# Two MLPs behind cluster attention on one core: the last two heads' values are multiplied with the tokens in columns

## The chip, the cores and the metric

One core of one Trainium2 chip runs the whole program. The metric is the device time of an execution in microseconds (us). TensorE is called PE here (its weight loads PEld), VectorE DVE, ScalarE ACT, GpSimd POOL, and SP is the engine that issues most DMAs. A line number such as L578 is that of the kernel before the change.

## The reference, cut to what matters

```
# q, k, v: 2 batches x 8 heads x 768 tokens x 64; 16 centroids per head
mask = q_assign[:, :, :, None] == k_assign[:, :, None, :]     # same nearest centroid
scores = where(mask, q @ k.T / 8, -1e9);  scores -= max(scores, -1)
attn = exp(scores);  attn = attn / (sum(attn, -1) + 1e-9)
x = (attn @ v) as 1536 tokens x 512                           # 8 heads side by side
x = gelu-like MLP(x): 512 -> 2048 -> 512
out = gated MLP(x):   512 -> 1536 (gate and value) -> 512
```

The 16 pairs of batch and head are called heads 0 to 15 below; heads 14 and 15 are the last two of batch 1.

## The kernel before

All five engines run an order that is written out by hand: each engine takes its instructions in the order of the Python code, and semaphores hold it where an operand or a buffer is not ready. Numbers are held as two float32r parts, a high one and a low rest, and a product is three matmuls (high by high, high by low, low by high).

A head goes through these steps. `next_smax` (matmul L531, maximum on DVE L536) finds the largest score of each query token of the *following* head, in 12 steps of 384 columns. `mneg` and `mrow` turn the maxima into one row of the query operand: a DVE reduce, a PE transposition into the bank `ps_x`, a copy on ACT and a DMA. `scores(h, c, n)` computes the scores of 128 key tokens (c, 0 to 5) by 384 query tokens (n, 0 and 1) with two matmuls (L578) into one of three banks `ps_s`, and ACT takes the exponential into `p` (L585). `pv(h, c)` (L594) then multiplies by the values: `p` is the stationary operand, 128 tokens at a time, and 65 columns of values (the 65th is ones, for the sums) stream, in float32. `norm` divides on DVE, with tokens on the partitions, and `to_x` (L625) transposes two heads at a time on PE back to features on the partitions and splits the result into `xh` (ACT, L631) and `xl` (DVE, L632).

In head 14 one `next_smax` stands behind each `scores`; in head 15 the twelve `scores` stand alone, since no head follows. After all scores of a head come its six `pv`. `take(4)` moves the decoding of weight tiles along (L81 and L83 on ACT, four steps L85 to L97 on DVE), and `run` splits decoded tiles into `sp` (ACT L160, DVE L161).

Then the first MLP starts. `m1_s1(0, f)` is one block of `h` matmuls (L167) for batch 0, in a part of 512 and one of 256 tokens, each into one of the two banks `ps_m`; tanh on ACT (L193), a multiply on DVE (L196) that frees the bank, a cast on ACT (L198) and a rest on DVE (L205) follow. Two blocks are computed ahead, and the last `to_x` stands within the first; then blocks of `a` matmuls and of `h` matmuls alternate to the end.

Of the kernel before, what the change touches and what calls it, by code (L numbers as in the profile page):

```python
# [8 lines left out]
F32 = mybir.dt.float32  # L9
# [16 lines left out]
def tile_cluster_attention_two_mlps(ctx: ExitStack, tc: tile.TileContext, qk, v, cen, w1, w2, wg, wv, w3, out):  # L26
# [18 lines left out]
    def pool(stack, name, bufs, **kw):  # L45
        return stack.enter_context(tc.tile_pool(name=name, bufs=bufs, reuse_waits="tile", **kw))
# [238 lines left out]
    with ExitStack() as att:  # L285
# [5 lines left out]
        ps_x = pool(att, "ps_x", 1, space=PSUM)  # L291
        ps_o = pool(att, "ps_o", 2, space=PSUM)
        ps_s = pool(att, "ps_s", 3, space=PSUM)
        qk_stack = ExitStack()
        qk_p = pool(qk_stack, "qk", 1)

# [7 lines left out]

        q2_t = [(qk1_p if i == FIRST else qk_p).tile([128, 2, S], F32R, name=f"q2_{i}") for i in range(NQK)]
        k2_t = [(qk1_p if i == FIRST else qk_p).tile([128, 2, S], F32R, name=f"k2_{i}") for i in range(NQK)]
# [263 lines left out]
        def scores(h, c, n):  # L572
            if n == 0:
                p_t[h, c] = p_p.tile([128, S], F32, tag="p", name="p")
            at = slice(n * HALF, (n + 1) * HALF)
            ps = ps_s.tile([128, 512], F32, tag="s", name="st")[:, 0:HALF]
            for a, rows in ((0, 2 * D), (1, MROW + 1)):
                nc.tensor.matmul(  # L578
                    out=ps,
                    lhsT=k2(h)[0:rows, a, c * 128:(c + 1) * 128],  # L580
                    rhs=q2(h)[0:rows, a, at],
                    start=(a == 0),
                    stop=(a == 1),
                )
# [119 lines left out]


        EARLY = 3
        for h in range(NH):
            more, ahead = h + 1 < NH, h + 4 < NH
            maxima = list(steps) if more and h > 1 else []
            for step in () if h == 0 else steps[2 * EARLY:] if h == 1 else steps:  # L710
                scores(h, *step)
                if maxima:
                    next_smax(h + 1, maxima)
            if h == 0:
                load_qk(5)
# [11 lines left out]
            if h == NH - 1:  # L727
                qk_stack.close()
                sp_p = pool(ctx, "sp", 6, side="right")
                g_p = pool(ctx, "gp", 3, side="right")  # L730
                w_pools.append(pool(ctx, "wd1", LATE, side="right"))
            for c in range(SC):
                if h or c:
                    pv(h, c)
                if more and c == 0:
                    if h > 1:
                        mrow(h + 1)
                    load_v(h + 1)
                    if ahead:
                        if h > 0:  # L740
                            hi_k(h + 4)
                            lo_q(h + 4, nc.gpsimd if h == 1 else nc.vector)
                            lo_k(h + 4, nc.gpsimd if h == 1 else nc.vector)
# [30 lines left out]
                if h == NH - 1 and c > 0:  # L774
                    run([], [[("1", 0)], [("1", 1), ("2", 0)], [("1", 2)], [("2", 1)], []][c - 1], 0)
# [8 lines left out]
            if h == NH - 1:  # L784
                norm(h)
# [76 lines left out]
```

## Time and profile before

| | before |
|---|---|
| median of 3 runs | 836.12 us (835.83 to 837.07) |
| profiled execution | 836.04 us, of which the trace spans 834.2 us |
| PE busy | 99% of the span, 4736 matmuls |
| DVE, ACT, POOL busy | 72%, 54%, 4% |
| granted TensorE clock, mean | 0.999 |

A matmul counts as busy from its start until its result is written, and matmuls overlap, so 99% does not say that PE is at its peak: the distance from one start to the next tells what a matmul costs. Times in the trace are counted from the start of the span. Head 14's first score matmul starts at 238.68, the first `h` matmul at 266.56 and the first `a` matmul at 276.36.

### The profile page before, as it was taken

To read this page: it belongs to the slowest core of one execution; us is meant where nothing else is said; L and a number is where in the kernel's file an instruction comes from. 1 tells how busy PE (TensorE), PEld (TensorE's weight loads), DVE (VectorE), ACT (ScalarE), POOL (GpSimd) and SP (SyncE) were. 2 spreads that over 40 slices of the span, in tenths; PEclk is the share of its full clock that TensorE was granted. 3 is DMA by queue.
4 is the path that set the end of the run, shared out by engine and by line. 5 is a ranking of instruction groups with operands and counts; after the bars stand their busy time and mean duration, and the time that the engine had idled before them with its cause. 6 is when DMAs were issued, how large, how long until landed. Compare 5 with 4: busy or idle time off the path is not lost.

```text
span 834.2 us, 12291 instructions
## 1 busy us (share of the span) xinstructions
PE 826.6 (99%) x4736; PEld 732.9 (88%) x4736; DVE 604.0 (72%) x1131; ACT 448.6 (54%) x828; POOL 36.4 (4%) x48
## 2 busy tenths in 40 slices
PE   8999999999999999999999999999999999999998
PEld 6999999999999888888888888888888888888886
DVE  7888898898973588888977776798965544555452
ACT  7847766766754465656654545565633333333331
POOL 8530000000000000000000000000000000000000
PEclk9999999999999999999999999999999999999999
DMA  6124123111211133333222222122201000010001
GB/s 127 31 81 110 37 55 88 35 54 50 66 50 47 51 101 112 116 102 112 91 76 83 70 98 80 51 79 99 75 1 51 1 0 1 1 51 0 1 1 50
DMA packets 26242, 49.79 MB, mean 60 GB/s; under 512 B 14548, under 2 KB 14632, under 8 KB 26184
## 3 DMA queue, kind: packets, MB, share of 16 engines
q1 hardware_dynamic: 25240, 47.24, 18.9%
q10 hardware_dynamic: 944, 1.77, 0.6%
q8 instruction: 37, 0.61, 0.3%
q14 instruction: 21, 0.17, 0.1%
HBM read 45.12 MB, written 3.15 MB: 58 GB/s over the span
## 4 chain that ended last, share of the span: by engine, by line
PE 94%; DVE 4%; ACT 1%; issue 1%; ACTq 0%; DVEq 0%
PE h L167 39%; PE a L167 28%; PE pv L594 13%; PE st L578 7%; PE smax L531 4%; DVE nm L536 1%; PE sims L447 1%; PE xt L625 0%; PE warm L366 0%; DVE k L349 0%; DVE q L343 0%; ACT p L585 0%; DVE oT L504 0%; DVE T L484 0%; DVE mx L482 0%
## 5 line engine op out<-in xcount | busy, mean ns | idle before, releaser
L167 PE MATMUL h<-xh,sp 128*128 128x512 f32 (+1 forms) x1088 | 313.9, 365 | 0.5 <-DVE t L196 0.5
L167 PEld LDWEIGHTS h<-xh,sp 128*128 128x128 f32 x1088 | 198.3, 189 | 33.8 <-issue 0.7
L167 PE MATMUL h<-xl,sp 128*128 128x512 f32 (+1 forms) x544 | 198.4, 365 | 0.0
L167 PE MATMUL a<-g,sp 128*128 128x512 f32 (+1 forms) x768 | 139.6, 338 | 0.0
L196 DVE SCALAR_TENSOR_TENSOR t<-t,h 128x512 f32<-128x512 f32 x100 | 60.0, 600 | 104.1 <-ACT t L193 104.1
L594 PEld LDWEIGHTS pv<-v,p 128*128 128x128 f32 x1152 | 134.8, 192 | 0.1
L167 PEld LDWEIGHTS a<-g,sp 128*128 128x128 f32 x768 | 120.0, 189 | 16.8
L594 PE MATMUL pv<-v,p 128*128 128x65 f32 x1152 | 134.3, 273 | 0.0
L193 ACT ACTIVATE t<-h 128x512 f32<-128x512 f32 x100 | 52.7, 527 | 144.8 <-PE h L167 144.8
L161 DVE TENSOR_TENSOR sp<-w,sp 128x512 fp32r<-128x512 f32 x172 | 115.4, 687 | 10.3 <-ACT sp L160 10.0
L167 PEld LDWEIGHTS h<-xl,sp 128*128 128x128 f32 x544 | 102.7, 189 | 16.2
L585 ACT ACTIVATE p<-st 128x384 f32<-128x384 f32 x192 | 89.9, 492 | 35.7 <-PE st L578 30.1
L160 ACT CAST sp<-w 128x512 fp32r<-128x512 f32 x172 | 101.9, 617 | 9.2 <-PE a L167 8.4
L167 PE MATMUL a<-sp,g 128*128 128x512 f32 x432 | 103.6, 389 | 0.0
L536 DVE TENSOR_REDUCE nm<-smax 128x1 f32<-128x384 f32 x192 | 98.0, 554 | 6.0 <-PE smax L531 5.6
L578 PE MATMUL st<-q,k 128*128 128x384 f32 (+1 forms) x384 | 98.4, 348 | 0.1
L167 PEld LDWEIGHTS a<-sp,g 128*128 128x128 f32 x432 | 81.1, 188 | 16.8
L205 DVE TENSOR_TENSOR g<-t,g 128x512 fp32r<-128x512 f32 x100 | 60.4, 604 | 28.7 <-ACT g L202 24.8
L202 ACT CAST g<-t 128x512 fp32r<-128x512 f32 x36 | 22.4, 623 | 97.4 <-DVE t L201 97.4
L578 PEld LDWEIGHTS st<-q,k 128*128 128x128 f32 (+1 forms) x384 | 67.3, 190 | 4.4 <-ACT p L585 2.7
L531 PE MATMUL smax<-k,q 80*128 80x384 f32 x192 | 62.9, 344 | 0.5 <-ACT q L507 0.2
L201 DVE TENSOR_TENSOR t<-t,h 128x512 f32<-128x512 f32 x36 | 24.8, 688 | 36.6 <-PE h L167 35.7
(99 smaller groups left out, 640.4 us busy)
## 6 DMA issues: line engine op xcount, KB each, us to landing
raw<-in_w SPq DMA_DIRECT2D x44, 512.0 KB, 3.2
raw<-in_wg SPq DMA_DIRECT2D x12, 512.0 KB, 3.1
raw<-in_wv SPq DMA_DIRECT2D x12, 512.0 KB, 3.5
st<-in_qk SPq DMA_DIRECT2D x15, 384.0 KB, 5.5
v<-in_v SPq DMA_DIRECT2D x16, 192.0 KB, 3.1
out<-osb ACTq DMA_DIRECT2D x6, 256.0 KB
out<-osb SPq DMA_DIRECT2D x6, 256.0 KB, 2.4
q<-oT SPq DMA_DIRECT2D x7, 48.0 KB, 2.2
```

What stands on the lines that cost most here:

```text
L160: lambda: nc.scalar.copy(t[:, 0, :], w),
L161: lambda: nc.vector.tensor_tensor(out=t[:, 1, :], in0=w, in1=t[:, 0, :].bitcast(F32), op=ALU.subtract),
L167: nc.tensor.matmul(out=out_ps, lhsT=lhs[a], rhs=rhs[b], start=(start and j == 0), stop=(stop and j == 2), **kw)
L193: nc.scalar.activation(t, hs[0], ACTF.Tanh, scale=tanh_scale)
L196: nc.vector.scalar_tensor_tensor(out=t, in0=t, scalar=1.0, in1=hs[0], op0=ALU.add, op1=ALU.mult)
L201: nc.vector.tensor_tensor(out=t, in0=t, in1=hs[1], op=ALU.mult)
L205: nc.vector.tensor_tensor(out=g[:, 1, at], in0=t, in1=g[:, 0, at].bitcast(F32), op=ALU.subtract)
L531: nc.tensor.matmul(out=ps, lhsT=q2(h)[0:ONE + NC, 1, c * 128:(c + 1) * 128], rhs=k2(h)[0:ONE + NC, 1, n * HALF:(n + 1) * HALF],)
L536: nc.vector.tensor_reduce(out=nm_t[h][:, c, n:n + 1], in_=ps, axis=AX.X, op=ALU.max)
L578: nc.tensor.matmul(out=ps, lhsT=k2(h)[0:rows, a, c * 128:(c + 1) * 128], rhs=q2(h)[0:rows, a, at], start=(a == 0), stop=(a == 1),)
L585: nc.scalar.activation(p_t[h, c][:, at], ps, ACTF.Exp, scale=scale)
L594: nc.tensor.matmul(out=pv_t[h][:, i, :], lhsT=p[:, i * 128:(i + 1) * 128], rhs=v_t[h % 3][:, c, :], start=(c == 0 and i == 0), stop=(c == ...
```

## The change

Only heads 14 and 15 and what follows them up to the first `a` block are changed.

- The values become the stationary operand: `split_v`, on POOL, builds a high and a low tile of 128 columns per 128 key tokens, 64 of them the values and 64 ones (zeros in the low tile). The exponentials stream: ACT copies each `p` into a high part `hi` (128x768), and POOL (head 14) or DVE (head 15) subtracts to get `lo`. `pvg` multiplies, three matmuls of 384 columns for each c and n. The result has features on 64 partitions, the sums on the other 64, and tokens in columns.
- Blocks of `pvg` stand behind the next scores: a list `todo` is worked off until two entries are left. Head 15's maxima are found two behind each `scores` of head 14, in its c = 0 to 2. `to_x` of heads 12 and 13, `mneg` and `mrow` stand among head 14's scores.
- `norm_g` divides in this layout: two DVE transposes bring the sums to columns, reciprocal, a broadcast copy on ACT, two transposes back, two multiplies. For head 14 its steps stand among head 15's scores, for head 15 among the first `m1_s1`. `split_x` takes the place of the last `to_x`, without PE.
- After the last scores, the remaining `pvg` run for n = 1 first, ACT copies that result out of its `ps_m` bank (`off_bank`), then n = 0.
- Two decodings move: from head 14, c = 1 and 4, to head 13, c = 3, and head 14, c = 5. Splits of `sp` stand behind head 15's exponentials instead of beside its `pv`. Pools are arranged so that the new tiles reuse buffers of heads 12 and 13.

```diff
@@ scores @@
             nc.scalar.activation(p_t[h, c][:, at], ps, ACTF.Exp, scale=scale)
+            if h >= NH - 2 and n == 1:
+                p = p_t.pop((h, c))
+                hi, lo = (q2_t, k2_t)[c // 2 % 2][U3][:, c % 2, :], p_p.tile([128, S], F32R, tag="p", name="lo")
+                hl_t[h, c] = hi, lo
+                nc.scalar.copy(hi, p)
+                (nc.gpsimd, nc.vector)[h % 2].tensor_tensor(out=lo, in0=p, in1=hi.bitcast(F32), op=ALU.subtract)
...
+        def pvg(h, c, low, ns=(0, 1)):
+
+            vh, vl = vs_t[h]
+            for n in ns:
+                if (h, n) not in pg_t:
+                    pl, tag = (ps_o, "o") if h % 2 == 0 else ((ps_x, "x"), (ps_m, "m"))[n]
+                    pg_t[h, n] = pl.tile([128, 512], F32, tag=tag, name="pg")[:, 0:HALF]
+                for w in (vh,) if low else (vh, vl):
+                    nc.tensor.matmul(
+                        out=pg_t[h, n], lhsT=w[:, c, :], rhs=hl_t[h, c][low][:, n * HALF:(n + 1) * HALF],
...
+        def norm_g(h):
...
+            for n in range(2):
+                nc.vector.transpose(out=d[:, n, :], in_=pg_t[h, n][sums])
+            yield
...
+            nc.vector.reciprocal(rd, rd)
+            nc.scalar.copy(d.rearrange("p n (b c) -> p n b c", c=32), rd.to_broadcast([64, 2, HALF // 32, 32]))
+            yield
+            for n in range(2):
+                nc.vector.transpose(out=r[rows, n * HALF:(n + 1) * HALF], in_=d[:, n, :])
+            yield
+            for n in range(2):
+                at = slice(n * HALF, (n + 1) * HALF)
+                nc.vector.tensor_tensor(out=x[rows, at], in0=pg_t[h, n][rows], in1=r[rows, at], op=ALU.mult)
+            yield
...
-        for at in ((NH - 4, 1), (NH - 4, 4), (NH - 3, 1), (NH - 2, 1), (NH - 2, 4)):
+        for at in ((NH - 4, 1), (NH - 4, 4), (NH - 3, 1), (NH - 3, 3), (NH - 2, 5)):
...
-        for h in range(NH):
+        for h in range(NH - 2):
...
+        maxima = list(steps)
+        todo = []
+        for h in (NH - 2, NH - 1):
+            for c in range(SC):
+                for n in range(2):
+                    scores(h, c, n)
+                    for _ in range(2 if maxima else 0):
+                        next_smax(NH - 1, maxima)
+                todo += [(h, c, False), (h, c - 1, True)] if c else [(h, c, False)]
...
+                    if c == 3:
+                        mneg(h + 1)
+                    if c == 4:
+                        mrow(h + 1)
+                    if c in (3, 4):
+                        to_x((h - 2) // 2, c - 3)
+                    take(takes.get((h, c), 0))
+                elif c > 1:
+                    next(after)
...
+                while len(todo) > 2:
+                    pvg(*todo.pop(0))
+                if h == NH - 1 and c == 1:
+                    after = norm_g(NH - 2)
...
+        last = norm_g(NH - 1)
         for i in range(2):
             for j, step in enumerate(m1_s1(0, i)):
                 step()
-                if i == 0 and j in (0, 3):
-                    to_x(NH // 2 - 1, j // 3)
+                if i == 0:
+                    next(last, None)
+                if i == 0 and j == 2:
+                    run([], [("1", 2)], 0)
+                if i == 1 and j in (0, 3):
+                    split_x(j // 3)
```

PE's order in head 14, c = 1 and 2 (`st` are the scores, `smax` the scores that are searched for head 15's maxima, `pg` the product with the values). Before:

```order
L578 MATMUL st_2860<-q2_4_118,k2_4_123 128x384 [waits Activation_49]
L578 MATMUL st_2860<-q2_4_118,k2_4_123 128x384
L531 MATMUL smax_2864<-k2_0_119,q2_0_114 128x384 [waits DVE_49]
L578 MATMUL st_2867<-q2_4_118,k2_4_123 128x384 [waits Activation_49]
L578 MATMUL st_2867<-q2_4_118,k2_4_123 128x384
L531 MATMUL smax_2871<-k2_0_119,q2_0_114 128x384 [waits DVE_49]
```

The same place on PE now (line numbers in these rows are those of the kernel they are from):

```order
L588 MATMUL st_2888<-q2_4_121,k2_4_126 128x384 [waits PE_49]
L588 MATMUL st_2888<-q2_4_121,k2_4_126 128x384
L541 MATMUL smax_2895<-k2_0_122,q2_0_117 128x384 [waits DVE_49]
L541 MATMUL smax_2898<-k2_0_122,q2_0_117 128x384 [waits DVE_49]
L632 MATMUL pg_2901<-q2_3_120,q2_2_119 128x384 [waits Activation_49,Pool_49]
L632 MATMUL pg_2901<-q2_3_120,q2_2_119 128x384 [waits Pool_49]
L632 MATMUL pg_2904<-q2_3_120,q2_2_119 128x384 [waits PE_49]
L632 MATMUL pg_2904<-q2_3_120,q2_2_119 128x384
L588 MATMUL st_2908<-q2_4_121,k2_4_126 128x384 x2
L541 MATMUL smax_2912<-k2_0_122,q2_0_117 128x384 [waits DVE_49]
L541 MATMUL smax_2915<-k2_0_122,q2_0_117 128x384 [waits DVE_49]
```

Two `smax`, each of which waits for a maximum on DVE, now stand between two pairs of scores, and the first product stands behind them in the same queue.

ACT's order in the last half of head 15 (`p` the exponentials, the casts from `p` are `hi`, `d` is the broadcast copy of head 14's reciprocal sums). Before, up to the first weight split:

```order
L585 ACTIVATE p_3019<-st_3020 128x384 [waits PE_49,Activation_49]
L585 ACTIVATE p_3019<-st_3024 128x384 [waits PE_49]
L585 ACTIVATE p_3028<-st_3029 128x384 [waits PE_49,Activation_49]
L585 ACTIVATE p_3028<-st_3033 128x384 [waits PE_49]
L585 ACTIVATE p_3037<-st_3038 128x384 [waits PE_49,Activation_49]
L585 ACTIVATE p_3037<-st_3042 128x384 [waits PE_49]
L160 CAST sp_3074<-w_1071 128x512
```

ACT now, from c = 3 to the end of head 15:

```order
L595 ACTIVATE p_3087<-st_3088 128x384 [waits PE_49]
L595 ACTIVATE p_3087<-st_3092 128x384 [waits PE_49]
L600 CAST k2_3_125<-p_3087 128x768 [waits Activation_49]
L663 COPY d_3077<-rdg_3099 64x768 [waits DMAHW7_49,DVE_49]
L595 ACTIVATE p_3109<-st_3110 128x384 [waits PE_49]
L595 ACTIVATE p_3109<-st_3114 128x384 [waits PE_49]
L600 CAST q2_3_120<-p_3109 128x768 [waits Activation_49]
L595 ACTIVATE p_3129<-st_3130 128x384 [waits PE_49]
L595 ACTIVATE p_3129<-st_3134 128x384 [waits PE_49]
L600 CAST q2_3_120<-p_3129 128x768 [waits Activation_49]
```

A cast of 768 columns now follows every two exponentials, and between c = 3 and c = 4 a copy that waits for DVE stands ahead of the last four exponentials.

DVE's order beside the first two `h` blocks (`t` and `g` are the MLP's gate; L196 frees the `h` bank). Before:

```order
L196 SCALAR_TENSOR_TENSOR t<-t,h 128x512
L205 TENSOR_TENSOR g<-t,g 128x512 [waits DMAHW7_49,DMAHW4_49,Activation_49]
L632 TENSOR_TENSOR xl_78<-xt,xh_77 128x256 [waits Activation_49]
L196 SCALAR_TENSOR_TENSOR t<-t,h 128x256
L205 TENSOR_TENSOR g<-t,g 128x256 [waits Activation_49]
```

DVE at the same place now:

```order
L196 SCALAR_TENSOR_TENSOR t<-t,h 128x512 [waits Activation_49]
L658 TENSOR_SCALAR rdg<-d 64x24 [waits DVE_49]
L662 RECIPROCAL rdg<-rdg 64x24 [waits DVE_49]
L205 TENSOR_TENSOR g<-t,g 128x512 [waits DMAHW1_49,Activation_49]
L666 STREAM_TRANSPOSE r<-d 64x384 [waits Activation_49]
L666 STREAM_TRANSPOSE r<-d 64x384
L161 TENSOR_TENSOR sp<-w,sp 128x512 [waits Activation_49]
L670 TENSOR_TENSOR xg<-pg,r 64x384 [waits DVE_49]
L670 TENSOR_TENSOR xg<-pgs,r 64x384 [waits DVE_49]
L196 SCALAR_TENSOR_TENSOR t<-t,h 128x256 [waits Activation_49]
L205 TENSOR_TENSOR g<-t,g 128x256 [waits Activation_49]
```

Between the two L196 that free the first block's two banks, DVE now has seven more instructions of head 15's division and of a weight split, where it had one.

## Rows read from the trace of the kernel before

**Rows 1.** Page, first part: busy us, share of the span, instructions.

```profile
PE 826.6 (99%) x4736; PEld 732.9 (88%) x4736; DVE 604.0 (72%) x1131; ACT 448.6 (54%) x828; POOL 36.4 (4%) x48
```

**Rows 2.** Chain that ended last, in order of time: start us, us, what.

```profile
210.17 5.95 DVE nm L536 x12
...
246.63 6.70 PE pv L594 x60
253.33 4.87 PE st L578 x24
...
263.51 0.44 PE xt L625 x4
...
265.24 0.23 PE xt L625 x2
...
270.75 0.54 issue
```

**Rows 3.** Busy time of each engine in stretches of heads 14 and 15.

```profile
core 0: us, PE busy (x) PEld busy (x) DVE busy (x) ACT busy (x) POOL busy (x), PEclk, DMA share, GB/s
238.68:245.12 6.44, 6.44 (x38) 6.44 (x38) 5.63 (x11) 5.28 (x11) 0.00 (x0) 1.00 0.00 0
245.12:253.14 8.02, 8.02 (x75) 8.02 (x74) 6.57 (x14) 3.29 (x7) 0.00 (x0) 1.00 0.48 153
...
238.68:276.36 37.68, 37.19 (x268) 34.89 (x268) 21.85 (x44) 20.34 (x43) 0.00 (x0) 1.00 0.11 34
```

**Rows 4.** Timeline of PE at the second h block and the first a block.

```profile
272.12 0.47 PE L167 MATMUL h<-xh,sp 128*128 128x512 f32 x1 [0.49 <-DVE t L196]
...
276.36 4.36 PE L167 MATMUL a<-g,sp 128*128 128x512 f32 x24
```

**Rows 5.** Timeline of ACT and DVE: start us, us, engine, line, instruction, count.

```profile
239.49 6.39 DVE L536 TENSOR_REDUCE nm<-smax 128x1 f32<-128x384 f32 x12 [1.04 <-PE smax L531]
...
246.00 0.15 DVE L611 TENSOR_SCALAR rd<-pv 128x6 f32<-128x6 f32 x1
...
246.41 0.56 DVE L613 TENSOR_TENSOR xr<-pv,rd 128x384 f32<-128x384 f32 x1
...
246.89 0.68 DVE L85 SCALAR_TENSOR_TENSOR u<-u,raw 128x512 f32<-128x512 f32 x1
...
248.79 0.69 DVE L97 CUSTOM_DVE_ANT_0 w<-m,t 128x1024 uint16<-128x1024 uint16 x1
...
253.77 4.98 ACT L585 ACTIVATE p<-st 128x384 f32<-128x384 f32 x12 [3.51 <-PE st L578]
...
263.99 0.59 ACT L631 CAST xh<-xt 128x512 fp32r<-128x512 f32 x1 [3.18 <-PE xt L625]
...
264.61 0.69 DVE L632 TENSOR_TENSOR xl<-xt,xh 128x512 fp32r<-128x512 f32 x1 [2.82 <-ACT xh L631]
...
269.57 0.60 ACT L193 ACTIVATE t<-h 128x512 f32<-128x512 f32 x1 [3.70 <-PE h L167]
...
271.29 0.68 DVE L196 SCALAR_TENSOR_TENSOR t<-t,h 128x512 f32<-128x512 f32 x1
272.00 0.62 ACT L198 CAST g<-t 128x512 fp32r<-128x512 f32 x1 [1.35 <-DVE t L196]
...
273.60 0.41 DVE L196 SCALAR_TENSOR_TENSOR t<-t,h 128x256 f32<-128x256 f32 x1
```

**Rows 6.** Groups by line, whole span: busy us, mean ns | idle before.

```profile
L338 ACT CAST k<-st 64x768 fp32r<-64x768 f32 x15 | 12.4, 830 | 0.1
L349 DVE TENSOR_TENSOR k<-st,k 64x768 fp32r<-64x768 f32 x11 | 10.5, 950 | 9.7 <-ACT k L338 9.5
L504 DVE STREAM_TRANSPOSE oT<-T 64x384 f32<-64x384 f32 x18 | 10.3, 572 | 0.7
L349 POOL TENSOR_TENSOR k<-st,k 64x768 fp32r<-64x768 f32 x5 | 9.1, 1826 | 0.4
```

**Rows 7.** Instructions on the tile k: duration ns min/median/max, start us.

```profile
L508 POOL CAST k<-oT x4: 497/530/1289, 12.4 to 24.4; 16x384 fp32r<-16x384 f32 x4
```

More of the change, by code (lines that the diff above doesn't have):

```diff
@@ L293, in tile_cluster_attention_two_mlps @@
         ps_s = pool(att, "ps_s", 3, space=PSUM)
+        qkb_stack = ExitStack()
+        qkb_p = pool(qkb_stack, "qkb", 1)
         qk_stack = ExitStack()
@@ L302, in tile_cluster_attention_two_mlps @@
         FIRST = (NH - NQK) % NQK
-        q2_t = [(qk1_p if i == FIRST else qk_p).tile([128, 2, S], F32R, name=f"q2_{i}") for i in range(NQK)]
-        k2_t = [(qk1_p if i == FIRST else qk_p).tile([128, 2, S], F32R, name=f"k2_{i}") for i in range(NQK)]
+        U2, U3 = ((NH - j) % NQK for j in (4, 3))
+        in_b = {("q", U3), ("k", U3), ("k", U2)}
+        q2_t, k2_t = (
+            [
+                (qk1_p if i == FIRST else qkb_p if (a, i) in in_b else qk_p).tile([128, 2, S], F32R, name=f"{a}2_{i}")
+                for i in range(NQK)
+            ]
+            for a in "qk"
+        )
         v_t = [acst.tile([128, SC, D + 1], F32, name=f"v_{i}") for i in range(3)]
@@ L585, in scores, with split_v @@
             nc.scalar.activation(p_t[h, c][:, at], ps, ACTF.Exp, scale=scale)
+            if h >= NH - 2 and n == 1:
[4 more added lines that the diff above has]
+                (nc.gpsimd, nc.vector)[h % 2].tensor_tensor(out=lo, in0=p, in1=hi.bitcast(F32), op=ALU.subtract)
+        hl_t = {}
+        vs_t = {}
+        def split_v(h):
+            dst = (q2_t, k2_t)[h % 2][U2]
+            vh, vl = (dst[:, i, :].rearrange("p (c d) -> p c d", d=2 * D) for i in range(2))
+            at, other = slice(0, D), slice(D, 2 * D)
+            if h % 2:
+                at, other = other, at
+            src = v_t[h % 3][:, :, 0:D]
+            nc.gpsimd.memset(vh[:, :, other].bitcast(F32), 1.0)
+            nc.gpsimd.memset(vl[:, :, other].bitcast(F32), 0.0)
+            nc.gpsimd.tensor_copy(vh[:, :, at], src)
+            nc.gpsimd.tensor_tensor(out=vl[:, :, at], in0=src, in1=vh[:, :, at].bitcast(F32), op=ALU.subtract)
+            vs_t[h] = vh, vl
@@ new lines, in tile_cluster_attention_two_mlps @@
+        pg_t = {}
+        def pvg(h, c, low, ns=(0, 1)):
[7 more added lines that the diff above has]
+                        out=pg_t[h, n], lhsT=w[:, c, :], rhs=hl_t[h, c][low][:, n * HALF:(n + 1) * HALF],
+                        start=(c == 0 and not low and w is vh), stop=(c == SC - 1 and low), skip_group_check=True,
+                    )
@@ new lines, in off_bank @@
+        def off_bank(h, n):
+            t = p_p.tile([128, S], F32, tag="p", name="pgs")[:, 0:HALF]
+            nc.scalar.copy(t, pg_t[h, n])
+            pg_t[h, n] = t
+        xg_t = []
+        def norm_g(h):
+            if not xg_t:
+                xg_t.append(xr_p.tile([128, SC, 2, D], F32, tag="xr", name="xg").rearrange("p a b d -> p (a b d)"))
+            x = xg_t[0]
+            rows, sums = slice(0, D), slice(D, 2 * D)
+            if h % 2:
+                rows, sums = sums, rows
+            d = am_p.tile([64, 2, HALF], F32, tag="oT", name="d")
+            r = p_p.tile([128, S], F32, tag="p", name="r")
+            for n in range(2):
+                nc.vector.transpose(out=d[:, n, :], in_=pg_t[h, n][sums])
+            yield
+            rd = sm_p.tile([64, 2, HALF // 32, 1], F32, tag="rdg", name="rdg")
+            nc.vector.tensor_scalar(
+                out=rd, in0=d.rearrange("p n (b c) -> p n b c", c=32)[:, :, :, 0:1],
+                scalar1=1e-9, scalar2=None, op0=ALU.add,
+            )
+            nc.vector.reciprocal(rd, rd)
[8 more added lines that the diff above has]
+            yield
@@ L587, in tile_cluster_attention_two_mlps, with split_x @@
+        def split_x(p):
+            t0, n = parts[p]
+            part, at = x_at(B - 1, p)
+            j = H // 2 - 1
+            x = xg_t[0][:, t0:t0 + n]
+            nc.scalar.copy(xh[part][:, j, at], x)
+            nc.vector.tensor_tensor(
+                out=xl[part][:, j, at], in0=x, in1=xh[part][:, j, at].bitcast(F32), op=ALU.subtract
+            )
         pv_t = {}
@@ L773, in tile_cluster_attention_two_mlps @@
                     norm(h - 1)
-                if h == NH - 1 and c > 0:
-                    run([], [[("1", 0)], [("1", 1), ("2", 0)], [("1", 2)], [("2", 1)], []][c - 1], 0)
+                if h == NH - 3 and c == 3:
+                    split_v(h + 1)
                 take(takes.get((h, c), 0))
@@ L783, in tile_cluster_attention_two_mlps @@
                         to_x((h - 3) // 2, c - 3)
-            if h == NH - 1:
-                norm(h)
+        maxima = list(steps)
[7 more added lines that the diff above has]
+                todo += [(h, c, False), (h, c - 1, True)] if c else [(h, c, False)]
+                if c == SC - 1:
+                    todo.append((h, c, True))
+                if h == NH - 2:
+                    if c == 0:
+                        norm(h - 1)
+                        load_v(h + 1)
+                    if c == 2:
+                        split_v(h + 1)
+                    if c == 3:
[7 more added lines that the diff above has]
+                    next(after)
+                if h == NH - 1 and c == SC - 1:
+                    break
+                while len(todo) > 2:
+                    pvg(*todo.pop(0))
+                if h == NH - 1 and c == 1:
+                    after = norm_g(NH - 2)
+        qk_stack.close()
+        sp_p = pool(ctx, "sp", 6, side="right")
+        run([], [("1", 0)], 0)
+        for n in (1, 0):
+            for at in todo:
+                pvg(*at, (n,))
+            if n == 1:
+                off_bank(NH - 1, n)
+        qkb_stack.close()
+        g_p = pool(ctx, "gp", 3, side="right")
+        w_pools.append(pool(ctx, "wd1", LATE, side="right"))
+        run([], [("1", 1), ("2", 0)], 0)
+        last = norm_g(NH - 1)
         for i in range(2):
@@ L788, in tile_cluster_attention_two_mlps @@
                 step()
-                if i == 0 and j in (0, 3):
-                    to_x(NH // 2 - 1, j // 3)
+                if i == 0:
[4 more added lines that the diff above has]
+                    split_x(j // 3)
+            if i == 0:
+                run([], [("2", 1)], 0)
     ps_a = pool(ctx, "ps_a", 1, space=PSUM)
```

5 lines of the change are left out of this document (removed).

## The prediction

> **What bounds the kernel now.** I read the page's busy times first: PE is busy for 99% of the span [rows 1], so what counts is what PE is made to do and where it waits. The windows of heads 14 and 15 show the granted clock at 1.00 and PE busy for 37.19 of the 37.68 us from head 14's first score (238.68, called T = 0 below) to the first `a` matmul (276.36, T = 37.68) [rows 3, 4]. Behind that point both kernels do the same work, `h` and `a` blocks back to back, so the change is worth what it moves the first `a` matmul. The chain that ended last then gives prices per matmul: 60 `pv` in 6.70 us, 0.112 each, and 24 score matmuls in 4.87 us, 0.406 a pair [rows 2]. That pair is not PE's own pace: twelve exponentials take 4.98 us on ACT [rows 5], so head 15's scores already wait for ACT. PE's own pace is read in head 14, where 24 score and 12 search matmuls, all of 384 columns, take 6.44 us: 0.179 each [rows 3]. Last I read the timeline of ACT and DVE, since the change gives these two the new work.
>
> **What the change takes from PE.** Removed: 144 `pv` matmuls (72 a head, 8.02 us in head 14's window [rows 3]) = 16.1 us, and the last six transpositions, 0.44 + 0.23 = 0.67 us [rows 2]. Added: 2 heads x 6 c x 2 n x 3 = 72 matmuls of 384 columns. No row has this form; the scores have the same columns and type, so 72 x 0.179 = 12.9 us (bounds: the `pv`'s 0.112 and 0.406/2 = 0.203, 8.1 to 14.6). PE alone would so need 132 x 0.179 = 23.6 us plus 0.8 for six transpositions and `mrow`, 24.4, to the first `h` matmul, which now stands at T = 27.88.
>
> **What it gives to ACT.** Twelve casts `hi` of 128x768. Nearest row: a cast of 64x768, 0.83 us [rows 6]; I take 0.83, between 0.62 for 128x512 [rows 5] and twice that. The cast waits for the second exponential itself. Twelve exponentials in 4.98 us are eleven starts of 0.41 and a last one of 0.49, so a block c costs ACT 0.41 + 0.49 + 0.83 = 1.73 us. PE's block (two pairs, six products) is 10 x 0.179 = 1.79. The two engines are thus level, and whatever holds either is not made up.
>
> **The chain, step by step.** It goes through queues that take their work in written order.
>
> 1. *Head 14, c = 0 to 2, DVE.* Search matmuls come two per pair of scores and have three banks, so each waits for the maximum three before it. The first maximum starts 0.81 after the scores (239.49) [rows 5]; where DVE sets the pace one costs 5.95/12 = 0.50 [rows 2]. Head 13's `norm`, 246.00 to 246.97 in the row of the next one, 0.97 us [rows 5], stands behind the fourth. The eighth search matmul waits for the fifth maximum: 0.81 + 5 x 0.50 + 0.97 = 4.3. Behind it stand four products, two pairs and three more searches, 12 matmuls with itself, 2.1 us; the twelfth comes at 6.6. ACT starves meanwhile.
> 2. *c = 3.* That search, six products and the next pair are 9 x 0.179 = 1.6: T = 8.2; an exponential starts 0.63 after its pair began (253.77 against 253.14 [rows 3, 5]), 0.28 after the pair's slot: 8.5. A block, 1.73: 10.2.
> 3. *c = 4.* `to_x` holds `ps_x` until `xh` (0.59) and `xl` (0.69) [rows 5] have read it: 11.5. `mrow` needs that bank and stands ahead of c = 4's products on PE. Then `mrow` and two transpositions 0.4, six products 1.1, a pair 0.35, exponential 0.28: 13.6.
> 4. *c = 5.* ACT's block to 15.4. PE has four products of this very block ahead of head 15's scores: 0.7 + 0.35 + 0.28, head 15's first exponential at 16.7.
> 5. *Head 15, c = 0 to 3.* ACT's blocks, 4 x 1.73: 23.6. The decoding moved to head 14, c = 5 (2.6 us on DVE, 246.89 to 249.48 [rows 5]) lies beside the first of them.
> 6. *The broadcast copy.* On ACT it stands ahead of c = 4 and waits for the reciprocal, which on DVE stands behind `lo` of c = 3, 0.95 us [rows 6]; adding and reciprocal 0.41 (246.00 to 246.41 [rows 5]): 25.0. The copy, priced as the 64x768 cast 0.83: 25.8.
> 7. *c = 4 and 5.* `hi` of c = 4 at 27.5, of c = 5 at 29.3. On DVE `lo` of c = 4 ends at 28.5, two transpositions of 0.57 [rows 6] at 29.6, the last `lo` at 30.6.
> 8. *PE's rest.* One product for n = 1 and seven for n = 0, 1.4: first `h` matmul at 32.0 (before: 27.88).
> 9. *First MLP.* In the kernel before, the second `h` block waits 0.49 us for L196 [rows 4], and the first `a` comes 9.80 after the first `h`. Now the second block's part of 256 tokens needs the bank that the second L196 frees, and DVE has head 15's division ahead of it. From the first `h`: tanh starts at 3.0 (269.57 - 266.56) and takes 0.60, L196 0.68, L198 0.62 [rows 5], broadcast copy 0.83 (behind L198 on ACT), transpositions 2 x 0.57, a weight split 0.69 (as `xl`), two multiplies 2 x 0.56 (as L613), L196 0.41: 9.1. PE would be there at about 7. That part is a third of the block's 4.24 us (272.12 to 276.36 [rows 4]), 1.4: first `a` at 10.4, given that queued instructions overlap a little.
>
> Sum: 32.0 + 10.4 = 42.4 against 37.68, **4.8 us later**. The profiled execution took 836.04, so 840.8; the median of the runs is 0.08 above it: **840.9 us**.
>
> **Costed at nothing.** POOL's six `lo` (1.83 each [rows 6], for half the partitions; bounds 1.8 and 3.7) and `split_v`, some 13.5 us from T = 2.8, are hidden behind 16 us of head 14, with about 2 to spare; at twice the price the products of head 15 would wait 9 us more, which I hold unlikely. The row's DMA for head 15 is issued near T = 13 and needed at 16.5; head 15's values load one step after head 14's first block and are needed by `split_v` some 4 us later. Head 13 gets one decoding more beside 8 us of `pv`. The weight splits that were hidden beside head 15's `pv` now run beside the last products; the first `h` needs its split's high part, ready before PE.
>
> **Rivals.**
>
> *PE's saving shows (faster).* If PE never waited, the first `h` came at 24.4 and the first `a` 2 x 4.2 later, 32.8: 4.9 earlier, 831.1. For it: ACT's block of 1.73 fits PE's 1.79. Against it: ACT also has `xh` twice, the row, two decoding steps and the copy, 3.4 us, and steps 1, 3 and 6. It decides if `hi` costs below about 0.5, so that ACT catches up behind each wait.
>
> *Only ACT's own work counts (no change).* With every wait covered, ACT needs 0.63 + 12 x 1.73 + 3.4 = 24.8 to the last `hi`, then 0.95 for `lo` and 1.4 on PE: first `h` at 27.2, with step 9 first `a` at 37.6, 0.1 earlier, 836.0. For it: the written order spreads the blocks evenly. Against it: the waits of steps 1, 3 and 6 stand in ACT's way in the order shown.
>
> *POOL and DVE block each other (slower still).* One cast on POOL took 1289 ns against a median of 530 [rows 7]. If DVE's decoding in step 5 stood behind POOL's last `lo`, which ends near T = 18, it would be 1.4 late; DVE has 0.8 to spare, so 0.6 more: 841.5. The Trainium skill's page "SBUF — State Buffer" (section "SBUF: two separate sides") says that DVE instructions with two SBUF inputs and POOL instructions that read SBUF exclude each other for the whole instruction. That rule would do just this here; the 1289 ns agree with it, but no row has two such instructions side by side.
>
> *The granted clock falls.* PE waits some 1 to 2 us in steps 3, 6 and 9; the longest wait in these heads before was about half a us, at 1.00 [rows 2, 3]. Were the 24 matmuls of head 15's last two blocks and rest taken at the lower level, that adds up to 24 x 0.179 = 4.3: 845.
>
> **Chances.** Forecast 0.68 (838 to 843.5 by its bounds), no change 0.12, faster 0.06, blocking 0.08, clock 0.06. Slower by over 0.2% (1.7 us, about what a measurement can tell) has 0.82, within 0.2% 0.12, faster 0.06. The range 836.0 to 844.0 takes in the forecast, the blocking and half of no change.
>
> **What would show it.** Right: ACT, not PE, busy without a gap in head 15; the copy idle for over 1 us behind DVE; PE waiting for DVE at the eighth search matmul, at `mrow` and at the second `h` block's 256 tokens; first `h` 32 us after head 14's first score. Wrong: products below 0.15 us apart, `hi` well below 0.83, PE without waits in head 15, or a first `a` less than 39 us after T = 0.

## Result: 842.0 us, 0.73% slower

The changed kernel takes 842.01 us (median of 5 runs, 841.39 to 843.38) against 836.12: a ratio of 1.0073, 95% interval 1.0058 to 1.0087. The forecast was 840.9, range 836 to 844. The profiled execution took 841.49, 5.45 more than the one of before.

The page's busy times of the changed kernel, as in [rows 1]:

```profile
PE 826.1 (98%) x4658; PEld 729.4 (87%) x4658; DVE 617.5 (74%) x1147; ACT 459.2 (55%) x843; POOL 52.9 (6%) x62
```

PE has 78 records fewer and only 0.5 us less busy time; its share falls from 99 to 98%. The windows say where (columns as in [rows 3]): head 14's first score to the first `h` matmul, from there to the first `a` matmul, two short stretches of head 15's end, and the whole.

```profile
238.67:271.60 32.93, 28.38 (x141) 24.52 (x141) 23.94 (x39) 25.20 (x46) 13.64 (x10) 0.95 0.07 20
271.60:282.14 10.54, 8.88 (x50) 7.36 (x50) 7.41 (x15) 4.31 (x9) 0.00 (x0) 1.00 0.01 2
266.00:268.00 2.00, 0.89 (x4) 0.57 (x4) 1.75 (x3) 1.97 (x5) 0.00 (x0) 0.99 0.00 0
268.00:271.40 3.40, 3.40 (x10) 3.06 (x11) 3.20 (x6) 1.89 (x4) 0.00 (x0) 0.51 0.00 0
...
238.67:282.14 43.47, 37.26 (x190) 31.88 (x190) 31.35 (x53) 29.51 (x55) 13.64 (x10) 0.96 0.05 16
```

The first `a` comes at T = 43.47 (T counts from head 14's first score, 238.67) against 37.68, 5.79 later. PE is busy 37.26 of these 43.47 us; before it was 37.19 of 37.68 [rows 3]. By the record PE's busy time hardly shrank, and PE now stands still for 6.2 us in which it has nothing to run. ACT isn't full either: 25.20 of the 32.93 us to the first `h`. For 3.4 us from 268.0 on the granted clock is at its lower level (0.51 of 2.4 GHz), behind two us in which PE was busy for 0.89. That stretch is part of the 37.26: in the kernel with four edits below, whose clock stays up, PE is busy for 35.17.

The timeline of PE, rows with a wait ahead of them, and the first `h` and `a`:

```profile
242.84 0.44 PE L541 MATMUL smax<-k,q 80*128 80x384 f32 x1 [0.85 <-DVE nm L546]
...
250.05 0.23 PE L573 MATMUL mrow<-ident_r,nr 128*6 128x128 f32 x1 [0.50 <-DVE xl L729]
...
253.80 0.97 PE L632 MATMUL pg<-q,q 128*128 128x384 f32 x4 [0.49 <-ACT q L600]
...
265.03 0.62 PE L588 MATMUL st<-q,k 128*128 128x384 f32 x2 [1.10 <-ACT p L595]
266.27 0.62 PE L632 MATMUL pg<-q,k 128*128 128x384 f32 x2 [0.61 <-ACT q L600]
...
267.90 0.99 PE L632 MATMUL pg<-q,k 128*128 128x384 f32 x2 [0.84 <-ACT q L600]
...
271.60 0.40 PE L167 MATMUL h<-xh,sp 128*128 128x512 f32 x1
...
280.60 0.39 PE L167 MATMUL h<-xh,sp 128*128 128x256 f32 x1 [1.67 <-DVE t L196]
```

The three waits of the prediction are there by name: the eighth search matmul for DVE's maxima, `mrow` for `xl` in `ps_x`, and the second `h` block's 256 tokens for L196. The wait on ACT for the broadcast copy shows on PE as the 1.10 at the last scores; the 0.61 and 0.84 behind it are waits for the last two `hi`. The same stretch on ACT, five rows: the first `hi`, head 15's first exponential, `hi` of c = 3, the copy, the last `hi`.

```profile
240.53 0.83 ACT L600 CAST q<-p 128x768 fp32r<-128x768 f32 x1
...
255.21 0.87 ACT L595 ACTIVATE p<-st 128x384 f32<-128x384 f32 x2 [0.32 <-PE st L588]
...
261.36 0.84 ACT L600 CAST k<-p 128x768 fp32r<-128x768 f32 x1
263.76 0.83 ACT L663 COPY d<-rdg 64x768 f32<-64x768 f32 x1 [1.57 <-DVE rdg L662]
...
267.02 0.83 ACT L600 CAST q<-p 128x768 fp32r<-128x768 f32 x1
```

And DVE's decoding beside GpSimd's last two `lo`, the timelines of both engines:

```profile
251.82 1.09 DVE L85 SCALAR_TENSOR_TENSOR u<-u,raw 128x512 f32<-128x512 f32 x1
252.95 1.94 DVE L89 TENSOR_SCALAR m<-u 128x512 int32<-128x512 int32 x1
254.92 2.22 DVE L93 SCALAR_TENSOR_TENSOR m<-u,m 128x512 int32<-128x512 int32 x1
...
252.33 4.25 POOL L601 TENSOR_TENSOR lo<-p,q 128x768 fp32r<-128x768 f32 x2
```

The first took 0.68 before [rows 5], and the whole decoding 2.6; here it takes 6.0 us (251.82 to 257.86), and GpSimd 2.12 for a `lo` against 1.84 for those before. DVE is late for head 15's first `lo` by 0.8, but no product waits for it in this kernel. GpSimd's last `lo` ends at 256.58, and the product that reads it starts at 256.63: it has nothing to spare.

### The profile page after: what moved, and what is told of

The parts are those of the page before. It is cut to its first block, busy times and chain, and to the rows that moved or that the text cites. A ratio compares the mean times of both kernels' runs of the same rounds, so it can differ in the third digit from the quotient of the medians.

```text
span 839.7 us, 12189 instructions
## 1 busy us (share of the span) xinstructions
PE 826.1 (98%) x4658; PEld 729.4 (87%) x4658; DVE 617.5 (74%) x1147; ACT 459.2 (55%) x843; POOL 52.9 (6%) x62
## 4 chain that ended last, share of the span: by engine, by line
PE 92%; DVE 5%; ACT 2%; issue 0%; POOL 0%; POOLq 0%; ACTq 0%; DVEq 0%
PE h L167 39%; PE a L167 28%; PE pv L691 11%; PE st L588 7%; PE smax L541 4%; DVE nm L546 2%; PE sims L457 1%; PE pg L632 1%; PE xt L722 0%; ACT p L595 0%; PE warm L376 0%; POOL lo L601 0%; POOLq L1000 0%; DVE k L359 0%; DVE q L353 0%
## 5 line engine op out<-in xcount | busy, mean ns | idle before, releaser
L196 DVE SCALAR_TENSOR_TENSOR t<-t,h 128x512 f32<-128x512 f32 x100 | 60.1, 601 | 103.3 <-ACT t L193 103.3
L691 PEld LDWEIGHTS pv<-v,p 128*128 128x128 f32 x1008 | 118.2, 192 | 0.1
L691 PE MATMUL pv<-v,p 128*128 128x65 f32 x1008 | 117.8, 273 | 0.0
```

Of the source, the lines that this page charges most:

```text
L196: nc.vector.scalar_tensor_tensor(out=t, in0=t, scalar=1.0, in1=hs[0], op0=ALU.add, op1=ALU.mult)
L691: nc.tensor.matmul(out=pv_t[h][:, i, :], lhsT=p[:, i * 128:(i + 1) * 128], rhs=v_t[h % 3][:, c, :], start=(c == 0 and i == 0), stop=(c == ...
```

## Experiments

The theory: what PE loses is waits that come from the written order of ACT, DVE and PE, on engines that each have time left (*waits*). The rivals: ACT's added casts alone are the bound (*work*), and the granted clock makes much of the loss (*clock*). Each kernel was timed in five rounds beside the kernel before, which took 836.01, 836.07 and 835.90 us in the three groups. T counts from head 14's first score in each kernel's own trace.

**One cause each.** The first four kernels change one place of the changed kernel.

*Broadcast copy of head 14 on GpSimd.*

```diff
-            nc.scalar.copy(d..., rd.to_broadcast(...))
+            (nc.scalar.copy, nc.gpsimd.tensor_copy)[h == NH - 2](d..., rd.to_broadcast(...))
```

> Head 14's broadcast copy of the reciprocal sums runs on POOL, which has nothing to do there, instead of on ACT ahead of head 15's c = 4. Theory of the waits (the written order holds ACT and PE): ACT's gap of 2.3 us between the cast of c = 3 and the exponentials of c = 4 closes, PE's wait of 1.1 us at the score matmuls of c = 5 with it, and the first `a` matmul comes 2 to 3 us earlier: about 839.5 against 842.0. Theory of the work (ACT's twelve added casts set the length, and each wait only moves): at most the 0.8 us of the copy itself, 841 or more.

Measured: 839.98 us, ratio 1.0042 (1.0029 to 1.0055). The first `h` is at T = 30.96 and the first `a` at 42.22. On PE's timeline the wait of 1.10 for the scores is gone:

```profile
265.54 0.62 PE L632 MATMUL pg<-q,k 128*128 128x384 f32 x2 [0.94 <-ACT q L600]
...
267.09 0.44 PE L632 MATMUL pg<-lo,k 128*128 128x384 f32 x1 [0.76 <-DVE lo L601]
```

What is left is the last block's own chain, exponential, `hi`, `lo`, product. The gain of the medians is 2.0, and 0.8 of it could be the copy's work as well as its wait. In the trace the first `h` comes 1.97 earlier and the first `a` 1.25: like the changed kernel's, this execution has 3.4 us at the lower clock, here from 267.5 on, and they reach into the first `h` block.

*Division of head 15 behind the second `h` block's tanh work.*

```diff
-                if i == 0:
+                if i == 0 and j in (0, 1, 4, 5):
                     next(last, None)
```

> The last two steps of head 15's division (transpositions back, multiplies) stand behind the second L196 on DVE instead of ahead of it. Theory of the waits: PE's wait of 1.67 us ahead of the second `h` block's 256 tokens goes, and the first `a` comes 1.4 to 1.7 us earlier, about 840.4. Rival: the wait only moves to the first `a` blocks, whose banks the division still reads, and the time stays at 842.

Measured: 841.35, ratio 1.0059 (1.0045 to 1.0073). From first `h` to first `a` it is 9.9 us in place of 10.54, about as before the change (9.80). The wait at L196 is gone, and a shorter one stands at the first `a` block, for the division:

```profile
282.82 3.38 PE L167 MATMUL a<-g,sp 128*128 128x512 f32 x18 [0.51 <-DVE xg L670]
```

This profiled execution had two stretches at the lower clock, at 243 and 270 us, so its T tells little.

*Searches one per pair of scores at n = 1, two at n = 0.*

```diff
-                    for _ in range(2 if maxima else 0):
+                    for _ in range(2 - n if maxima else 0):
```

> Head 15's twelve search matmuls stand two and one in turn behind the scores of c = 0 to 3 instead of two each in c = 0 to 2. Theory of the waits: PE's waits for DVE's maxima, 0.85 us at the eighth search and some 0.4 in small ones, go, and 0.5 to 1 us of it reaches the first `a`: about 841.3. Theory of the work: ACT makes the time up later, 842.0.

Measured: 841.1, ratio 1.0061 (1.0048 to 1.0073). The search's wait of 0.85 is gone, a shorter one comes at the first transpositions, which need the bank of a later search:

```profile
246.45 0.65 PE L722 MATMUL xt<-ident,xr 128*128 128x128 f32 x4 [0.41 <-DVE nm L546]
```

The first `h` is at T = 31.77, 1.16 earlier, but the first `a` at 43.49 is no earlier than in the changed kernel. In this execution 6.8 us from 266.0 on were at the lower clock, twice as much as there, so its trace doesn't show what of the gain is left.

*Row of maxima through a bank of its own.*

```diff
-                        mrow(h + 1)
+                        mrow(h + 1, ps_m, "m")
```

> The matmul that turns head 15's maxima into a row writes a bank of `ps_m`, which is free there, instead of `ps_x`. Theory of the waits: its 0.50 us wait for the rest of the transposed block goes, and 0.3 to 0.5 us of it reaches the first `a`: about 841.6. Theory of the work: 842.0.

Measured: 841.73, ratio 1.0068 (1.0056 to 1.0081), not told apart from the changed kernel. The wait at `mrow` is gone, and the next thing in line takes its place, a product that waits for GpSimd's last `lo`:

```profile
256.58 0.62 PE L632 MATMUL pg<-lo,q 128*128 128x384 f32 x2 [0.65 <-POOL lo L601]
```

Only the first of the four has an interval that lies below the changed kernel's. Together they do not stay so small.

**All four together.**

> All four of the single edits together: broadcast copy of head 14 on GpSimd, division of head 15 put off behind the second h block's tanh work, searches spread one per pair, the row of maxima through its own bank. Waits theory (the written order holds ACT at each of these places, and ACT's block of about 1.73 us never makes it up): the gains add, 2.5 (copy) + 0.9 (search) + 0.5 to 0.9 (row) + 0.6 (division), first a about 4.5 us earlier than in the changed kernel, T = 39 and 836.5 to 837.5 us, just above the kernel before. Work theory (ACT's own work in head 15, 12 casts of 0.83, is the bound whatever the waits): the gains overlap and the time stays at 839 or more, and ACT is busy without a gap over the whole of the two heads. Clock rival: if the lower granted clock comes from PE's waits, this kernel has less of it, and its runs at 1.00 are the majority.

Measured: 836.53 us, ratio 1.0011 (1.0002 to 1.0019): 5.5 of the 5.9 us are gone. The gains of the four single medians add up to 3.9. Eight of the eleven runs had a mean granted clock of 0.999 or 1.0, where none of the changed kernel's five had more than 0.997. PE's timeline, all its waits of over 0.3 us from head 14's first score to the first `a`, and the window of that stretch:

```profile
246.39 0.66 PE L724 MATMUL xt<-ident,xr 128*128 128x128 f32 x4 [0.43 <-DVE nm L546]
...
252.40 0.98 PE L632 MATMUL pg<-q,q 128*128 128x384 f32 x4 [0.49 <-ACT q L600]
...
264.29 0.61 PE L632 MATMUL pg<-q,k 128*128 128x384 f32 x2 [0.94 <-ACT q L600]
...
265.83 0.44 PE L632 MATMUL pg<-lo,k 128*128 128x384 f32 x1 [0.76 <-DVE lo L601]
...
277.04 1.17 PE L167 MATMUL a<-g,sp 128*128 128x512 f32 x5 [0.52 <-DVE xg L672]
...
238.53:277.04 38.51, 35.17 (x189) 30.51 (x189) 30.18 (x52) 28.75 (x53) 14.28 (x11) 1.00 0.07 22
```

ACT still makes all twelve `hi`. The time is the one that the waits theory gave (836.5 to 837.5), and the work theory (839 or more) falls. But its 5.5 us are not the waits' alone: the clock stays up as well, and the next kernel tells what that is worth.

**The clock.** Matmuls whose result nobody reads, put into PE's waits; all of the changed kernel's work stays.

```diff
+        def fill(ps, n):
+            for _ in range(n):
+                nc.tensor.matmul(out=ps, lhsT=cs[:, 0, 0:128], rhs=cs[:, 0, 0:512])
...
+                    if h == NH - 1 and c > 3:
+                        fill(fill_m, ((4, 2), (0, 2))[c - 4][n])
```

> The changed kernel with matmuls that serve nothing put where PE waits in heads 14 and 15 (3 of 512 columns at the search wait, 2 at the row, 12 about the copy and the last casts); they lie inside the waits by the trace, so the chain that sets the end is meant to stay. If the drop of the granted clock to the lower level near T = 29 comes of those waits: no row at the lower level between T = 27 and 35, products 0.18 apart to the end, first h at T = 32 and not 33, all runs at one clock, 1 to 1.5 us less than the changed kernel: 840 to 840.5. If the drop comes whatever PE does there, or is not worth what I put on it: 842, spread as before. If the fills don't fit the waits, each costs up to 0.24 us more.

Measured: 840.45, ratio 1.0052 (1.0038 to 1.0065), and its five runs lie between 840.15 and 840.54, all at a clock of 0.999 or 1.0, where the changed kernel's five are spread over 2.0 us at 0.995 to 0.997. The same two stretches of head 15's end in its windows, and the whole:

```profile
266.00:268.00 2.00, 1.71 (x8) 1.07 (x7) 1.72 (x3) 1.97 (x5) 0.00 (x0) 1.00 0.00 0
268.00:271.40 3.40, 3.28 (x16) 2.78 (x17) 3.37 (x7) 1.93 (x4) 0.00 (x0) 1.00 0.00 0
238.68:281.12 42.44, 39.59 (x206) 33.59 (x206) 31.27 (x53) 29.54 (x55) 13.65 (x10) 1.00 0.05 16
```

With PE busy 1.71 of the two us ahead, the clock stays at 1.00. The first `h` is at T = 31.89 and the first `a` at 42.44, where the prediction had 32.0 and 42.4. The drop is thus worth 1.0 us in the trace and 1.6 in the medians. From here to the kernel with the four edits, at the same clock, it is 3.9 us: that is what the four edits take from the waits. It equals the sum of the four medians, which is in part chance, since those kernels had stretches at the lower clock of differing length. For the copy alone there is a comparison at one clock: its two runs at 1.0 took 838.6, 1.9 less than this kernel.

**Relieving ACT.** If ACT's work were the bound, taking casts off it should gain most.

*`hi` of head 15 on DVE.*

```diff
-                nc.scalar.copy(hi, p)
+                (nc.scalar.copy, nc.vector.tensor_copy)[h % 2](hi, p)
```

> The casts hi of head 15 are made by DVE, which also makes their lo; nothing else changes. Work theory (ACT's 0.83 per block in head 15 is what makes PE's saving vanish): ACT's block falls to 0.9, PE's own 1.79 becomes the bound, first h at T = 29, first a at T = 40, about 838 us. Waits theory (what counts are the three waits in written order, of which the copy now stands behind more DVE work: hi and lo of one block are 1.8 us on DVE, the copy waits for both of c = 3): first h no earlier than T = 31.5, 840.5 to 842 us.

Measured: 844.27, ratio 1.0097 (1.0084 to 1.0111): slower than either theory allowed. A cast costs DVE 0.55, cheaper than ACT's 0.83, but it stands in DVE's order. DVE's rows:

```profile
255.07 2.21 DVE L93 SCALAR_TENSOR_TENSOR m<-u,m 128x512 int32<-128x512 int32 x1
257.31 0.69 DVE L97 CUSTOM_DVE_ANT_0 w<-m,t 128x1024 uint16<-128x1024 uint16 x1
257.92 0.55 DVE L600 CAST q<-p 128x768 fp32r<-128x768 f32 x1
...
265.12 0.29 DVE L662 RECIPROCAL rdg<-rdg 64x24 f32<-64x24 f32 x1
```

The first `hi` waits for the decoding that GpSimd stretches (PE waits 1.14 there), and the reciprocal comes 1.7 later than in the changed kernel (265.12 against 263.44), with ACT's copy and the last two blocks of scores behind it. The first `h` is at T = 35.06. Here too 6.8 us were at the lower clock, from 268.5 on, so not all of the 2.3 us by which this kernel is slower than the changed one need be DVE's order itself.

*The four edits and this one.*

> The four single edits and hi of head 15 on DVE together. If waits and work are both needed to explain the loss and both are removed: PE runs without a wait of over 0.5 us from head 14's scores to the first h, first h at T = 26 to 27, first a at T = 36.5 to 37.5, 835 to 836 us, equal to the kernel before or a little below it. If DVE now becomes the bound (1.8 us per block in head 15 beside the division's transpositions): first h at T = 29 or later, 838 us. PE's saving in full (831) is expected by neither.

Measured: 840.34, ratio 1.005 (1.0037 to 1.0063), 3.8 worse than the four edits without it. Neither time that was stated came. The sign for DVE as the bound did, a first `h` at T = 29 or later (33.10), and PE's two longest waits are for DVE:

```profile
257.31 1.10 PE L632 MATMUL pg<-q,k 128*128 128x384 f32 x4 [1.60 <-DVE q L600]
...
268.19 0.99 PE L632 MATMUL pg<-q,k 128*128 128x384 f32 x2 [1.87 <-DVE q L600]
```

This execution had two stretches of over 3 us at the lower clock, at 258 and 268 us, and no run of this kernel was above 0.998, so a part of the 3.8 may be the clock. How much was not measured.

*`hi` and `lo` of head 14's c = 3 to 5 on DVE, alone.*

```diff
-                nc.scalar.copy(hi, p)
-                (nc.gpsimd, nc.vector)[h % 2].tensor_tensor(out=lo, ...)
+                dve = h == NH - 2 and c > 2
+                (nc.vector.tensor_copy if dve else nc.scalar.copy)(hi, p)
+                (nc.vector if dve or h % 2 else nc.gpsimd).tensor_tensor(out=lo, ...)
```

> In head 14, c = 3 to 5, hi and lo are made by DVE, which is idle there, in place of ACT (3 x 0.83) and GpSimd; nothing else changes in the changed kernel. Work theory: ACT has 2.5 us less to do ahead of head 15's last block, the first h comes 1.7 to 2.5 earlier, T = 30.5 to 31.2, about 839.5. Waits theory: the wait at the row of maxima (T = 11.4) and the four products ahead of head 15's first scores stay, and those hold ACT, not its own casts: head 15's first exponential 0.3 to 0.5 earlier than 16.54, first h T = 32.5 at the same clock, 841.5.

Measured: 843.72, ratio 1.0096 (1.0082 to 1.0111), 1.7 slower than the changed kernel, which neither theory had in its numbers. DVE's rows, and what PE made of them:

```profile
247.82 1.51 DVE L601 CAST k<-p 128x768 fp32r<-128x768 f32 x1 [1.46 <-ACT p L595]
249.43 1.06 DVE L602 TENSOR_TENSOR lo<-p,k 128x768 fp32r<-128x768 f32 x1
250.42 0.15 DVE L557 TENSOR_REDUCE nr<-nm 128x6 fp32r<-128x12 f32 x1
...
251.22 0.23 PE L573 MATMUL mrow<-ident_r,nr 128*6 128x128 f32 x1 [1.81 <-DVE xl L730]
```

The cast and `lo` were written ahead of `nr`, the reduction that `mrow` reads. It now comes at 250.42, in the changed kernel at 246.53, and `xl` behind it; `mrow` waits 1.81 in place of 0.50. The cast takes 1.51 beside GpSimd's work on the values, and 0.56 where GpSimd is silent. The profiled execution had 6.8 us at the lower clock from 267.7 on, twice the changed kernel's, so the 1.7 may be in part the clock.

**What is left at both ends of head 15.** Two kernels on top of the four edits. The first eases its start: the DVE edit just shown, the transpositions of the last full pair behind the products, and

```diff
-        ..., (NH - 3, 1), (NH - 3, 3), (NH - 2, 5)):
+        ..., (NH - 3, 1), (NH - 3, 3), (NH - 3, 5)):
...
-                while len(todo) > 2:
+                while len(todo) > 2 + (h == NH - 2 and c == SC - 1):
```

> The four single edits, and what still holds the start of head 15: hi and lo of head 14's c = 3 to 5 on DVE, the last decoding one step of head 13 earlier, the transpositions of the last full pair behind the products, and head 15's first scores ahead of the four products of head 14's last block. By waits theory head 15's first exponential, 253.77 in the kernel with the four edits (T = 15.2), comes at T = 13.7 to 14, and all behind it with it: first h at T = 27.3 to 27.6, first a 37.0 to 37.3, 835.0 to 835.4. If PE's own pace (1.79 a block) is by now the bound in head 15: the first h no earlier than 28.3, 836.

Measured: 837.62, ratio 1.0024 (1.0015 to 1.0034), 1.1 worse than the four edits alone. PE's wait, and the window of five blocks of head 15, c = 0 to 4:

```profile
251.37 0.23 PE L573 MATMUL mrow<-ident_r,nr 128*6 128x128 f32 x1 [1.69 <-DVE nr L557]
...
255.09:263.81 8.72, 8.72 (x52) 8.59 (x50) 5.95 (x9) 8.50 (x15) 0.12 (x1) 1.00 0.00 0
```

The start was lost to the wait at `mrow`, since the last maximum and `nr` again stand behind a cast and a `lo` on DVE, and to 0.97 at a search (T = 2.80), where the decoding moved into head 13 makes DVE late. Behind it PE is busy for all of 8.72 us and ACT for 8.50: in head 15 the two engines are level, at 1.70 a block for ACT and 1.74 for PE, as the prediction's 1.73 and 1.79 had it.

The other kernel halves the last block: the second 384 tokens' scores first, `hi` and `lo` of each half right behind its exponential.

```diff
+            if (h, c) == (NH - 1, SC - 1):
...
+                nc.scalar.copy(hi[:, at], p[:, at])
+                nc.vector.tensor_tensor(out=lo[:, at], in0=p[:, at], in1=hi[:, at].bitcast(F32), op=ALU.subtract)
...
-                for n in range(2):
+                for n in (1, 0) if (h, c) == (NH - 1, SC - 1) else (0, 1):
                     scores(h, c, n)
```

> The four single edits, and the last block of head 15 in halves: the scores of its second 384 tokens first, hi and lo of each half right behind its exponential. In the kernel with the four edits PE waits 0.94 for this block's hi and 0.76 for its lo; half of the cast and of lo is 0.4 and 0.45 less. Expected: both waits under 0.4, first h at T = 27.5 to 27.9, first a 37.2 to 37.6, 835.2 to 835.7. If the fixed costs of the smaller instructions on ACT eat it: T = 28.5 and 836.2.

Measured: 836.14, ratio 1.0003 (0.9994 to 1.0011): the kernel before, within what can be measured. The wait for `hi` shrank as meant, the one for `lo` grew from 0.76 to 0.94:

```profile
263.65 0.62 PE L639 MATMUL pg<-q,k 128*128 128x384 f32 x2 [0.25 <-ACT q L601]
...
265.48 0.45 PE L639 MATMUL pg<-lo,k 128*128 128x384 f32 x1 [0.94 <-DVE lo L602]
```

The first `h` is at T = 28.36 and the first `a` at 38.10, each 0.4 earlier than with the four edits alone, where 0.9 to 1.3 was expected.

*Both together.*

> All edits of the two kernels beside it together. If the gains add (start of head 15 1.3 earlier, tail 1.1 shorter): first h at T = 26.3 to 26.6, first a 36.0 to 36.4, 834.0 to 834.6, below the kernel before by 0.2%. If PE is the bound by then (132 matmuls of 0.179, 24.4 with no wait at all): no more than one of the two gains, 835. The saving of PE in full (831) stays out, since the division ahead of L196 keeps the second h block's wait or the first a's.

Measured: 837.48, ratio 1.0019 (1.001 to 1.0028). The gains didn't add, since the first part has none: `mrow` waits 0.92 for `nr` here, and the search at T = 2.81 waits 0.97 as well. None of the kernels run beats the one before.

## Why the prediction was right

The direction, the size and the way were right: the first `a` 5.79 later where 4.8 was forecast (its own sum, 42.4 less 37.68, is 4.7), and 4.76 later (42.44) with the clock held up. Step by step, T of the changed kernel's trace against the forecast:

- *Steps 1 and 2.* Eighth search matmul 4.17 (4.3), exponential of c = 3 at 8.4 (8.5). The search wait is real: its own kernel took it away. What it is worth alone isn't shown: the first `h` came 1.2 earlier but the first `a` did not, and the 0.9 of the medians lies within the intervals.
- *Step 3.* `mrow` 11.38 (11.5). Right about the wait, but it is worth little: with its bank freed, GpSimd's `lo` held PE instead.
- *Step 4.* Head 15's first exponential 16.54 (16.7).
- *Step 5.* `hi` of c = 3 ends at 23.53 (23.6), `hi` being 0.83 to 0.84 as taken from the cast of 64x768.
- *Step 6.* Copy from 25.09 to 25.92 (25.0 to 25.8). Confirmed as the dearest of the causes, 1.9 us at one clock and 2.0 in the medians.
- *Step 7.* Last `hi` ends at 29.18 (29.3), last `lo` at 30.32 (30.6).
- *Step 8.* First `h` 32.93 (32.0). This is the one step that was off: it priced the last products at 0.179 each, and ten matmuls of that end ran in the 3.4 us at the lower clock. With the clock held up the first `h` is at 31.89. The "granted clock falls" rival, given 0.06, came true in part. Ten and not 24 matmuls fell into it, 1.8 us by the rival's own price in place of 4.3, and 1.0 of it reached the first `a`.
- *Step 9.* From first `h` to first `a` 10.54 (10.4), the wait 1.67 at the 256 tokens. Confirmed by the later division (9.9).

Of the signs named, all but one came. "ACT, not PE, busy without a gap in head 15" came by half: in its c = 0 to 3 (255.21 to 262.20, 6.99 us) ACT is busy for 6.63 and PE for 6.84, so neither alone sets the pace there.

"PE's saving shows" didn't come: PE waited where it would have saved. But its premise is seen in the kernel that eased the start, where products run at PE's pace. "Only ACT's own work counts" failed as a forecast, since its condition, that every wait is covered, didn't hold. Its sum for a kernel without those waits, 836.0, is near what came once most of them were gone: 836.53 with the four edits and 836.14 with the last block halved. So even the mended change gains nothing: between the waits that are left (0.43 to 0.94 each) ACT's blocks in head 15 are as long as PE's. That no other order of these instructions would gain is not shown. What the four edits refute is the work theory of the experiments, that ACT's casts hold the time at 839 whatever the waits: they give back 3.9 us at one clock and take 0.83 of work off ACT. That ACT's casts cost nothing is not shown by that; every kernel that relieved ACT did so on DVE, and made new waits there. Casts on GpSimd were not tried.

One term costed at nothing was too kind: GpSimd's `lo` were to be hidden "with about 2 to spare". Their price was right (1.84 for 1.83), but the last one ends 0.05 ahead of the product that reads it, and with the row's wait gone PE waits 0.65 for it.

"POOL and DVE block each other" is in the rows (6.0 us for 2.6), and costs the changed kernel nothing that a wait shows, so its 0.6 did not come. The Trainium skill's page "SBUF — State Buffer" (section "SBUF: two separate sides") says that a DVE instruction with two SBUF inputs and a GpSimd instruction that reads SBUF exclude each other, so that the one that comes second is blocked for as long as the other runs. The trace agrees: DVE's L93, with two inputs, took 2.22 beside a `lo` of 2.12 on GpSimd, and 0.69 where GpSimd was silent (in the kernel with head 14's casts on DVE). The 1289 ns of the prediction are no such case, since DVE ran a cast with one input beside that one (L334, 24.42 to 25.37). In the kernel with head 15's `hi` on DVE the stretched decoding held up the first `hi`.

In the median, 842.01 is 1.1 above the forecast; with the clock held up it is 840.45, 0.4 below it. All kernels of the experiments win back 0.2 to 0.3 us between the first `a` and the end (557.84 us before, 557.56 in the changed one), which the forecast did not have; the cause stays open.

## What to carry to other kernels

A shorter stream on the busiest engine gained nothing here, where every block of it came to hang on three other engines. So price the chain through their written order first, not only the sum of each engine's work. Look for the one small instruction (a reciprocal, a row of maxima, a broadcast copy) that stands behind a long one on its engine and ahead of the next block on another: the four moves in the written order gave back 3.9 us at one clock, while every kernel that moved casts to DVE lost time. Work put on an engine that idles in the sums still takes a place in its order: the casts moved to DVE came ahead of something that PE waited for. And before two kernels are compared, look at the granted clock in each trace: several of the kernels compared here ran longer at the lower clock than their partner.

## What the hardware showed unexpectedly

The granted clock fell to 1.2 GHz for 3.4 us behind two us in which PE was busy 0.89, and no single wait of PE in head 15 was longer than 1.10 us. With useless matmuls in the waits it stayed at 2.4 GHz, and the spread of the runs fell from 2.0 us to 0.4. A cast of 128x768 took DVE 0.55 us where GpSimd was silent and 1.51 beside the end of GpSimd's `lo`, two memsets and a cast; GpSimd's own cast there took 0.82 in place of 0.51. GpSimd made the broadcast copy of 64x768 in 0.82 us, as fast as ACT (0.83).
